# Retention and PReLU MLP on one core: fewer bytes of loads under way at first, one weight piece finished by halves, the last output block sent by quarters

## The chip, the cores and the metric

The kernel runs on one core of one Trainium2 chip. A core has a matrix engine (PE in the profile; PEld is its weight load), three elementwise engines (DVE, ACT, POOL), SyncE (SP), which here only starts transfers, and 16 DMA engines between the chip's main memory and the on-chip SBUF. Matmul results go to PSUM, a small memory that POOL does not read in this kernel. The metric is the device time of one execution in microseconds (us): 1020.53 us, the median of three runs from 1019.59 to 1022.61. The profile is of a fourth execution of 1020.18 us; its span, from the first to the last instruction, is 1018.5 us, and all instants below count from the span's start.

## The reference

```python
# q, k, v: (8, 8, 576, 64) float32
scores = matmul(q, k.T) / sqrt(64)
gamma  = 1 - 2.0 ** (-5 - arange(8))                 # one decay per head
Dmat   = where(i >= j, gamma ** (i - j), 0)          # per head, 576 x 576
x      = matmul(scores * Dmat, v)                    # then (B,H,S,D) -> (4608, 512)
h = x @ w_in                                         # w_in (512, 2048), float64
g = maximum(h, 0) + alpha * minimum(h, 0)            # alpha (2048,)
out = g @ w_out                                      # w_out (2048, 512), float64; out float32
```

## The kernel before

**Retention.** It is computed in chunks of 64 positions: within a chunk by masked scores, across chunks by a running sum of k-times-v states that decays by gamma. The powers of gamma are tables built at the start on DVE. Batch 0, the first 576 tokens, is handled in three parts of 256, 256 and 64 tokens, all eight heads at once, by the `part_*` functions; the other batches go by pairs of heads.

**MLP.** The 4608 tokens form 18 blocks of 256. A block goes through 8 units; unit i makes two 128-row pieces of h (matmuls into `ph`), applies the PReLU into `g`, and adds `g` times the rows of w_out into the block's output sums in PSUM (`po`, `mlp_out`). Blocks 0 and 1 are "plain" (L412 `plain_unit`, L390 `plain_out`). The other 16 use seven products of half-size operands instead of eight, from sums of weights and of x (L451 `mlp_unit`, L380). When a block's last unit is in, `out_block` (L355) combines the seven sums into the four 128x256 quarters `osb[m][x]` of the output and sends each 128-token row m as one 256 KB transfer (L369 to L371).

**Weights.** Both weights are float64 and are turned into float32 on the chip by 32 pieces, in the order in which the units use them: for unit i two pieces of w_in (each of two loads of 256 KB) and two of w_out (one load of 512 KB each). Pieces 0 and 1 together hold unit 0 of w_in; piece 2 and 3 its rows of w_out. `piece_in` (L285) runs two ACT instructions on a loaded piece (L296, L298); `piece_out` (L301) runs three DVE instructions through one PSUM buffer `c` (L307, L310, L312) and one on POOL (L314), and asks for the next load (`fetch`).

**Loads.** Nearly all loads are started by SP, which works through its list in order. `load` (L77) makes a load wait until the one that lies `in_flight` bytes back in the list has landed: it adds sizes backwards from the new load, itself included, and waits for the first earlier load before which the sum has reached the limit. The limit is 5 x 256 KB at first (L90), 7 x 256 KB from L827 on, and none from L889 on. The list begins with k and v of part 0 (two loads of 256 KB each), pieces 0 to 5, k, q, v of part 1 (six of 256 KB), then, under the second limit, pieces 6 and 7 and part 2. The two loads of part 0's q and the small alpha go out on ACT's queue (L161, L167) and are not counted.

**Order.** From L134 to L942 every engine runs its instructions in the order in which the code calls for them. Around the change it is (L830 to L863): scale, transpose and score part 0; `piece_in(1)`; states of part 0 (four ACT copies at L744, three POOL sums at L746); `piece_in(2)`; `piece_out(2)`, which is where pieces 0 and 1 are finished; the values of part 0 (PE at L764 and L775, then six ACT copies at L781 and L783 that fill `xb[0]`, the first three of them its first half); `piece_out(1)`; `piece_in(2)`, `piece_out(1)`; `plain_unit(0, 0)`. The last makes 8 matmuls at L419, each of which the trace shows as two: the first four use piece 0 and the first half of `xb[0]`, the next two the first half of piece 1, the last two its second half. Later the order of each engine comes from a scheduler.

Of the kernel before, what the change touches and what calls it, by code (L numbers as in the profile page):

```python
# [10 lines left out]
FP32 = mybir.dt.float32  # L11
INT32 = mybir.dt.int32
UINT32 = mybir.dt.uint32
ACTF = mybir.ActivationFunctionType
ALU = mybir.AluOpType
# [3 lines left out]
def kernel(  # L19
# [10 lines left out]
    nc = tc.nc  # L30
# [3 lines left out]
    P = 128  # L34
# [9 lines left out]
    HM = DM // 2  # L44
    TB = 2 * P
    NKB = NTOK // TB
# [40 lines left out]
                ahead += n  # L87
            flight.append((ins, size))

    in_flight = [5 << 18]  # L90

# [99 lines left out]
    for i in range(NBIT - 1):  # L193
        nc.vector.scalar_tensor_tensor(out=dif[:, i + 1], in0=dif[:, i], scalar=2.0,
                                       in1=dif[:, i], op0=ALU.add, op1=ALU.mult)
# [6 lines left out]
                            op=ALU.mult)  # L202
    nc.vector.tensor_scalar(pf, pf, 1.0, None, ALU.add)

    for o, x, y in ((slice(0, 2), slice(0, 2), slice(3, 5)), (0, 0, 1), (0, 0, 2), (1, 0, 5)):
# [7 lines left out]
                                   in1=pf[:, 6], op0=ALU.mult, op1=ALU.mult)  # L213
# [17 lines left out]
    for h2 in range(2):  # L231
# [6 lines left out]
                                       in1=tabx[hd, :, 0], op0=ALU.add, op1=ALU.mult)  # L238
# [13 lines left out]
    HI_MAX = float(np.array([0x47EFFFFF], np.uint32).view(np.float32)[0])  # L252
    HI_MIN = float(np.array([0x38000000], np.uint32).view(np.float32)[0])
# [10 lines left out]
    def fetch(n):  # L264
        while npiece[0] < min(n, len(pieces)):
            srcs, at = pieces[npiece[0]][0], npiece[0]
            npiece[0] += 1
            free[:] = [t for t in free if at < gone.get(t, len(pieces))]
            t = free.pop(0)
            if isinstance(t, str):  # L270
                raw = ring.tile([P, 4 * HM], INT32, tag=t, name=f"raw_{at}")
            else:
                raw = w_in[t][:, 4:6].rearrange("p s u c f -> p (s u c f)").bitcast(INT32)
            for i, src in enumerate(srcs):
                to = raw
                if len(srcs) > 1:
                    to = raw.rearrange("p (x e f two) -> p x e f two", x=2, e=2, two=2)[:, :, i]
                load(to, src, P * 4 * HM * 4 // len(srcs))
            raws.append((raw, t))
# [21 lines left out]
    def piece_out(n):  # L301
        for _ in range(min(n, len(half_done))):
            at, a, lo, hi, t = half_done.pop(0)
            dst = pieces[at][1]

            c = ps_h.tile([P, 2, HM], INT32, tag="psh1", name=f"wc_{at}")
            nc.vector.tensor_scalar(c.bitcast(FP32), a, HI_MIN, HI_MAX, ALU.max, ALU.min)  # L307


            nc.vector.tensor_scalar(c, c, 3, 0x3FFFFFF8,  # L310
                                    ALU.logical_shift_left, ALU.bitwise_and)
            nc.vector.scalar_tensor_tensor(out=dst.bitcast(INT32), in0=hi, scalar=-0x40000000,  # L312
                                           in1=c, op0=ALU.bitwise_and, op1=ALU.bitwise_or)
            nc.gpsimd.tensor_tensor(out=dst.bitcast(INT32), in0=dst.bitcast(INT32), in1=lo,  # L314
                                    op=ALU.add)
            free.append(t)
            fetch(at + 1 + AHEAD)

# [36 lines left out]
    def out_block(kb, po):  # L355
        p1, p2, p6, p7, p5, p3, p4 = [po[n // 2][:, n % 2, :] for n in range(7)]

        osb = ring.tile([P, 2, 2, HM], FP32, tag=f"o{kb % 2}", name=f"osb_{kb}")
        s12 = wraw.tile([P, 2, HM], FP32, tag="wa", name=f"s12_{kb}")
        u3 = wraw.tile([P, HM], FP32, tag="wa", name=f"u3_{kb}")  # L360
        s1, u2 = s12[:, 0], s12[:, 1]
        nc.scalar.copy(s1, p1)
        for o, x, y, op in ((osb[:, 0, 0], p2, s1, ALU.add), (u2, p6, s1, ALU.add),
                            (u3, p7, u2, ALU.add), (s1, p5, u2, ALU.add),
                            (osb[:, 1, 1], p5, u3, ALU.add),
                            (osb[:, 0, 1], p3, s1, ALU.add)):
            nc.vector.tensor_tensor(out=o, in0=x, in1=y, op=op)
        nc.vector.tensor_tensor(out=osb[:, 1, 0], in0=p4, in1=u3, op=ALU.add)
        for m in range(2):  # L369
            t0 = kb * TB + m * P  # L370
            nc.sync.dma_start(out[t0:t0 + P, :], osb[:, m].rearrange("p x f -> p (x f)"))  # L371

    def mlp_out(between=None):
        kb, i, g = pend.pop(0)
        if kb in PLAIN:
            return plain_out(kb, i, g, between)
        if i == 0:
            acc[kb] = [ps_o.tile([P, 2, HM], FP32, tag=f"pso{n}", name=f"po{n}_{kb}")
                       for n in range(4)]
        for n, (x, y) in enumerate(PROD):  # L380
            nc.tensor.matmul(acc[kb][n // 2][:, n % 2, :], g[:, x, :], w_out[i][:, y, :],  # L381
                             start=(i == 0 and n % 2 == 0),
                             stop=(i == NU - 1 and (n % 2 == 1 or n == 6)),
                             skip_group_check=True)
        if i == NU - 1:
            out_block(kb, acc.pop(kb))
# [449 lines left out]
    part_states(0)  # L836
    piece_in(2)
    piece_out(2)
    part_carry(0)
    part_values(0)  # L840
    aps = ps_a.tile([P, NFC], FP32, tag="psa", name="aps")
    nc.tensor.transpose(aps, a16, ident[0:NFC, 0:NFC])
    piece_out(1)
    nc.vector.tensor_copy(alpha, aps)
    nc.vector.tensor_scalar(nalpha, alpha, -1.0, None, ALU.mult)
    piece_in(2)
    piece_out(1)
    part_scale(1, 1)
    plain_unit(0, 0)
# [97 lines left out]
    for b in range(2, B):  # L947


        nq, first, at = len(queue), b * NPAIR, {}  # L950
# [56 lines left out]
```

## Time and profile before

| what | value |
|---|---|
| PE busy | 1001.3 us, 98% of the span |
| DVE, ACT, POOL busy | 778.3, 269.4, 179.2 us |
| DMA | 64.30 MB, mean 63 GB/s; up to 238 GB/s in a fortieth of the span |
| PE in the forty slices | 0.6 busy in the first, 0.7 in the last, 0.9 or more in each between |
| chain that ended last | PE 94%, DVE 3%, DMA 1% |
| output transfers | 36 of 256 KB, median 2.3 us from issue to landing |

The page gives busy time per engine, the span in forty slices, the DMA queues, the chain of work that ended last (followed back from the end, at each step to what released it), and the costliest groups of instructions. Since PE is busy nearly everywhere from about 42 us to the last block, a query of the trace by stages is needed to see the beginning and the end, which is where the change acts. `in_flight` and the order of pieces only matter while weights are being loaded; the tail is what lies behind the last matmul.

### The profile page before, as it was taken

What the parts mean: (1) busy time and instruction counts of PE and PEld (TensorE: products, weight loads), DVE (VectorE), ACT (ScalarE), POOL (GpSimd) and SP (SyncE); (2) the same over time, 40 slices, a digit from 0 to 9 for tenths busy, and PEclk for the clock granted to TensorE, in tenths of its full rate; (3) what the DMA queues carried; (4) which work ended last, traced back from release to release, by engine and by line L of the source; (5) the groups of instructions that cost most, each with busy time, mean ns of one, the idle gap of its engine ahead of it and who ended that gap; (6) DMA issues with size and microseconds to landing.
All of it is one profiled execution on the core that took longest, in us unless ns stands there. A gap on an engine that the chain in (4) does not pass through costs nothing.

```text
span 1018.5 us, 23084 instructions
## 1 busy us (share of the span) xinstructions
PE 1001.3 (98%) x9385; PEld 894.2 (88%) x9385; DVE 778.3 (76%) x2086; ACT 269.4 (26%) x605; POOL 179.2 (18%) x201
## 2 busy tenths in 40 slices
PE   6999999999999999999999999999999999999997
PEld 5666668899999999999999999999999999999997
DVE  6669966878887888768778788887878777667665
ACT  4556653223222222122021312232222211000000
POOL 5656674300100020100010000200020001010000
PEclk8999999999999999999999999999999999999999
DMA  9975744322231323112112313222313000000000
GB/s 238 238 194 140 185 74 103 60 60 48 52 64 40 63 37 69 25 45 48 44 25 56 60 45 60 57 48 54 62 45 60 13 23 1 22 1 21 2 21 22
DMA packets 229308, 64.30 MB, mean 63 GB/s; under 512 B 214337, under 2 KB 222545, under 8 KB 229201
## 3 DMA queue, kind: packets, MB, share of 16 engines
q1 hardware_dynamic: 227088, 62.29, 27.1%
q8 instruction: 74, 1.21, 0.5%
q10 hardware_dynamic: 2112, 0.53, 0.3%
q14 instruction: 34, 0.27, 0.1%
HBM read 53.35 MB, written 9.44 MB: 62 GB/s over the span
## 4 chain that ended last, share of the span: by engine, by line
PE 94%; DVE 3%; DMA 1%; ACT 0%; issue 0%; SPq 0%; POOL 0%; DVEq 0%; ACTq 0%
PE ph L463 38%; PE po L381 37%; PE ph L419 6%; PE po L398 6%; PE pv L656 3%; PE ps L614 1%; PE ps L620 1%; DMA w_out<-in_k_dram 1%; PE ph L614 1%; DVE su L589 0%; DVE g L476 0%; PE pt L697 0%; DVE mt L636 0%; PE ps L716 0%; PE ps L556 0%
## 5 line engine op out<-in xcount | busy, mean ns | idle before, releaser
L381 PE MATMUL po<-w_out,g 128*128 128x256 f32 x1792 | 410.9, 381 | 0.2
L381 PEld LDWEIGHTS po<-w_out,g 128*128 128x128 f32 x1792 | 330.1, 190 | 42.7 <-DVE g L487 1.3
L476 DVE TENSOR_TENSOR g<-ph,g 128x256 f32<-128x256 f32 (+1 forms) x512 | 187.0, 386 | 127.2 <-ACT g L471 75.2
L463 PE MATMUL ph<-xb,w_in 128*128 128x128 f32 x2048 | 272.7, 276 | 0.0
L463 PEld LDWEIGHTS ph<-xb,w_in 128*128 128x128 f32 x2048 | 257.1, 192 | 7.9 <-issue 0.7
L463 PE MATMUL ph<-xt,w_in 128*128 128x128 f32 x1536 | 213.8, 275 | 0.7 <-DVE g L476 0.7
L463 PEld LDWEIGHTS ph<-xt,w_in 128*128 128x128 f32 x1536 | 192.2, 192 | 1.1 <-PE ph L463 0.8
L487 DVE TENSOR_TENSOR g<-g 128x128 f32<-128x128 f32 x512 | 127.2, 289 | 5.4
L471 ACT COPY g<-ph 128x128 f32<-128x128 f32 x128 | 34.1, 266 | 327.7 <-PE ph L463 217.1
L528 POOL TENSOR_TENSOR qx<-qx,tabx 128x576 f32<-128x576 f32 x28 | 32.3, 1153 | 379.6 <-DMA qx<-in_q_dram 223.4
L481 DVE SCALAR_TENSOR_TENSOR g<-g 128x512 f32<-128x512 f32 x128 | 91.3, 714 | 3.8
L479 DVE TENSOR_SCALAR g<-g,alpha 128x256 f32<-128x256 f32 x256 | 84.3, 370 | 2.8
L597 ACT COPY vn<-su 64x512 f32<-64x512 f32 x56 | 34.6, 617 | 135.2 <-DVE su L591 134.5
L419 PE MATMUL ph<-xb,w_in 128*128 128x256 f32 x256 | 61.7, 397 | 0.8 <-POOL w_in L314 0.8
L419 PEld LDWEIGHTS ph<-xb,w_in 128*128 128x128 f32 x256 | 50.1, 198 | 11.0 <-issue 2.4
L398 PE MATMUL po<-w_out,g 128*128 128x512 f32 x128 | 58.6, 599 | 0.9 <-DVE g L435 0.9
L625 DVE SCALAR_TENSOR_TENSOR mt<-ph,th,mask 64x64 f32<-64x64 f32 x48 | 13.6, 283 | 52.5 <-PE ph L614 52.2
L665 ACT COPY xb<-pv 128x256 f32<-128x256 f32 (+3 forms) x84 | 22.7, 321 | 109.8 <-PE pv L656 109.8
L636 DVE SCALAR_TENSOR_TENSOR mt<-ps,th,mask 64x256 f32<-64x256 f32 x96 | 46.1, 481 | 2.3
L533 ACT ACTIVATE vn<-vn,tabv 64x576 f32<-64x576 f32 x56 | 43.3, 774 | 8.7 <-DMA vn<-in_v_dram 7.8
L398 PEld LDWEIGHTS po<-w_out,g 128*128 128x128 f32 x128 | 23.4, 190 | 24.5 <-issue 22.9
L589 DVE SCALAR_TENSOR_TENSOR su<-su,gch 128x64 f32<-128x64 f32 x84 | 43.1, 513 | 2.1
(134 smaller groups left out, 717.0 us busy)
## 6 DMA issues: line engine op xcount, KB each, us to landing
out_dram<-osb SPq DMA_DIRECT2D x36, 256.0 KB, 2.3
kx<-in_k_dram SPq DMA_DIRECT2D x112, 72.0 KB, 2.6
qx<-in_q_dram SPq DMA_DIRECT2D x112, 72.0 KB, 3.0
vn<-in_v_dram SPq DMA_DIRECT2D x56, 144.0 KB, 3.2
kn<-in_k_dram SPq DMA_DIRECT2D x56, 144.0 KB, 3.3
raw<-in_moe_w_in_dram SPq DMA_DIRECT2D x24, 256.0 KB, 4.5
raw<-in_moe_w_out_dram SPq DMA_DIRECT2D x10, 512.0 KB, 5.4
w_in<-in_moe_w_out_dram SPq DMA_DIRECT2D x6, 512.0 KB, 5.7
```

Of the source, the lines that this page charges most:

```text
L381: nc.tensor.matmul(acc[kb][n // 2][:, n % 2, :], g[:, x, :], w_out[i][:, y, :], start=(i == 0 and n % 2 == 0), stop=(i == NU - 1 and (n % ...
L398: nc.tensor.matmul(acc[kb][m], g[:, 2 * x + m], w_out[i][:, 2 * x:2 * x + 2].rearrange("p x f -> p (x f)"), start=(i == 0 and x == 0), sto ...
L419: nc.tensor.matmul(ph[:, x], w_in[i // UST][:, cc // 2 * 2 + x, i % UST, cc % 2], xb[kb][:, cc], start=(cc == 0 and x == 0), stop=(cc == N ...
L463: nc.tensor.matmul(ph[m][:, o], w_in[i // UST][:, l, i % UST, cc], r[:, cc], start=(n in (0, 3) and cc == 0), stop=(n in (2, 6) and cc == ...
L476: nc.vector.tensor_tensor(out=o, in0=x0, in1=x1, op=ALU.add)
L479: nc.vector.tensor_scalar(g[:, 4 + 2 * m:6 + 2 * m], g[:, 2 * m:2 * m + 2], 0.0, alpha[:, fc:fc + 1], ALU.min, ALU.mult)
L481: nc.vector.scalar_tensor_tensor(out=g[:, 0:4].rearrange("p x t -> p (x t)"), in0=g[:, 0:4].rearrange("p x t -> p (x t)"), scalar=0.0, in1 ...
L487: ins = nc.vector.tensor_tensor(out=g[:, o, :], in0=g[:, x0, :], in1=g[:, x1, :], op=op)
L533: nc.scalar.activation(vn[x, h2], vn[x, h2], ACTF.Copy, scale=tabv[x, c:c + 1])
L589: nc.vector.scalar_tensor_tensor(out=su[:, j], in0=su[:, j - 2], scalar=g2, in1=su[:, j], op0=ALU.mult, op1=ALU.add)
L597: nc.scalar.copy(vn[half(h2), h2, 1:], su[half(h2)])
L636: nc.vector.scalar_tensor_tensor(out=mt[to, h2, p2:NJ - 1:2], in0=ps[p2][half(x), 0], scalar=th[to, 3, h:h + 1], in1=mask[to, None, :].to_ ...
```

## The change

It has three parts. The limit on loads under way at first becomes 3 x 256 KB (0.75 MB) instead of 1.25 MB; the later limit is the same. Piece 1 is finished by its two column halves, so that a matmul may wait for the half that it uses: three DVE instructions and one of POOL become six and two of half the size. The last block's four quarters each go out as soon as they are there, as 128 KB transfers, two on SP's queue and two on ACT's, instead of two rows of 256 KB on SP's. The first two are for the beginning, so that what is needed first has less beside it and the first matmuls of the MLP wait for less; the third is for the end.

```diff
-    in_flight = [5 << 18]
+    in_flight = [3 << 18]
...
             c = ps_h.tile([P, 2, HM], INT32, tag="psh1", name=f"wc_{at}")
-            nc.vector.tensor_scalar(c.bitcast(FP32), a, HI_MIN, HI_MAX, ALU.max, ALU.min)
-            nc.vector.tensor_scalar(c, c, 3, 0x3FFFFFF8,
-                                    ALU.logical_shift_left, ALU.bitwise_and)
-            nc.vector.scalar_tensor_tensor(out=dst.bitcast(INT32), in0=hi, scalar=-0x40000000,
-                                           in1=c, op0=ALU.bitwise_and, op1=ALU.bitwise_or)
-            nc.gpsimd.tensor_tensor(out=dst.bitcast(INT32), in0=dst.bitcast(INT32), in1=lo,
-                                    op=ALU.add)
+            for f in (slice(0, P), slice(P, HM)) if at == 1 else (slice(0, HM),):
+                dst_e, c_e, a_e, hi_e, lo_e = [y[:, :, f] for y in (dst, c, a, hi, lo)]
+                nc.vector.tensor_scalar(c_e.bitcast(FP32), a_e, HI_MIN, HI_MAX, ALU.max, ALU.min)
+                nc.vector.tensor_scalar(c_e, c_e, 3, 0x3FFFFFF8,
+                                        ALU.logical_shift_left, ALU.bitwise_and)
+                nc.vector.scalar_tensor_tensor(out=dst_e.bitcast(INT32), in0=hi_e,
+                                               scalar=-0x40000000, in1=c_e,
+                                               op0=ALU.bitwise_and, op1=ALU.bitwise_or)
+                nc.gpsimd.tensor_tensor(out=dst_e.bitcast(INT32), in0=dst_e.bitcast(INT32),
+                                        in1=lo_e, op=ALU.add)
...
         nc.vector.tensor_tensor(out=osb[:, 1, 0], in0=p4, in1=u3, op=ALU.add)
+        if kb == NKB - 1:
+            for (m, x), eng in (((0, 0), nc.sync), ((1, 1), nc.scalar), ((0, 1), nc.sync),
+                                ((1, 0), nc.scalar)):
+                t0 = kb * TB + m * P
+                eng.dma_start(out[t0:t0 + P, x * HM:(x + 1) * HM], osb[:, m, x])
+            return
         for m in range(2):
```

Each engine's order of instructions is the same in both kernels but for these: six DVE and two POOL instructions in place of three and one, and the four output transfers. What changes beyond them is what SP's early loads wait for.

## The prediction

> **What bounds the kernel now.** I read the page's busy times first, then the slices, the chain of waits, stages of the beginning, and the tail.
>
> ```profile
> PE 1001.3 (98%) x9385; PEld 894.2 (88%) x9385; DVE 778.3 (76%) x2086; ACT 269.4 (26%) x605; POOL 179.2 (18%) x201
> ...
> PE   6999999999999999999999999999999999999997
> ```
>
> PE is the bound: 1018.5 - 1001.3 leaves 17 us without PE, and the slices put them at the two ends. From 60 to 110 us the stages show PE busy 50.00 of 50 us. So a microsecond that PE gains or loses in the first 40 us reaches the end whole, and so does one behind the last matmul; nothing else counts. The chain of waits over the first 120 us, and the timeline of the first 60:
>
> ```profile
> 1.31 5.78 DMA w_out<-in_k_dram
> 17.89 1.29 POOL w_in L314
> 19.18 0.08 issue
> 19.26 6.76 PE ph L419 x16
> 34.36 3.65 PE ph L419 x16
> ```
> ```profile
> 17.13 1.21 PE L775 MATMUL pv<-pT,w_out 64*32 64x64 f32 x82 [2.13 <-issue]
> 17.96 0.37 ACT L781 COPY xb<-pv 128x256 f32<-128x256 f32 x1 [1.47 <-PE pv L775]
> 18.37 0.74 ACT L783 COPY xb<-pv 64x256 f32<-64x256 f32 x2
> ```
>
> Three things are seen. The same 16 matmuls of L419 take 6.76 us at 19.26 and 3.65 us at 34.36. Before them PE stands 2.13 us (15.00 to 17.13) for nothing that the profile shows. And L419 is charged to piece 1 (POOL, 19.18), but ACT's copies of the first half of `xb[0]`, which the first matmul needs as well, end at 18.37 + 0.74 = 19.11. The first matmul uses piece 0, which POOL finished at 17.31. So I hold the copies, not piece 1, for the releaser. The stages say why L419 is slow (columns: stretch, its length, PE, PEld, DVE, ACT, POOL busy, granted clock, DMA share, GB/s):
>
> ```profile
> 15.20:18.62 3.42, 1.37 (x83) 1.17 (x82) 3.10 (x6) 1.92 (x5) 2.77 (x4) 1.00 0.91 308
> 18.62:22.03 3.41, 2.77 (x7) 2.26 (x8) 2.61 (x6) 3.33 (x9) 2.44 (x3) 0.50 1.00 251
> 22.03:25.45 3.42, 3.42 (x10) 2.70 (x9) 1.09 (x2) 0.61 (x2) 2.17 (x2) 0.50 0.98 215
> 25.45:28.86 3.41, 2.50 (x14) 1.71 (x13) 1.66 (x4) 2.82 (x6) 1.12 (x2) 1.00 0.98 282
> ```
>
> The clock is halved from 18.62 to 25.45, 6.83 us, after a stretch in which PE was busy 1.37 of 3.42 us. The tail, from the timeline of the end:
>
> ```profile
> 1013.98 0.41 DVE L368 TENSOR_TENSOR osb<-po,u 128x256 f32<-128x256 f32 x1
> 1014.09 1.08 SPq L371 DMA_DIRECT2D out_dram<-osb  x2
> ```
>
> The last sum ends at 1014.39, the second row's issue starts at 1014.83 and lands at 1017.36 (2.53 us); 1.1 us of final barriers follow.
>
> **What the Trainium skill says.** (1) "TensorE: Matmul & The Clock Gate", Part 1: the matrix clock is halved when an activity monitor finds the engine idle, in free-running windows of 3413 ns, so that the instant varies from run to run. The trace agrees: both changes lie on a grid of 3.41 us, 6.83 us apart. (2) "Runtime: NRT & Kernel Launch", Instruction fetch mechanics: each engine fetches its instructions by a DMA queue of its own in 16 KiB blocks of 256, mostly hidden. Here it seems not to be hidden: the page has 74 instruction packets of 1.21 MB on q8; a packet of 16,384 bytes runs from 14.79 to 15.75, and PE resumes 1.38 us later. PE's only other wait of this kind ends at 40.59, 1.49 us after the end of such a packet. (3) "DMA: Bandwidth & Descriptors", Issuing engines are not separate DMA queues: a second issuing engine saves the sequencer's issue time only. The trace has it as 0.33 us for each of the last two issues.
>
> **Part 1, the limit.** It removes nothing from SP's list; each 256 KB load now waits for the third before it instead of the fifth. The first three loads are unaffected, and in the records the bytes of both k loads and both q loads are in by 6.9 us, with less than 0.04 MB of v among them. So the first chain (k at 7.08, q at about 7.9, POOL scaling, transposes, scores at 10.11) gains nothing; I charge 0. Then I rebuilt the landings from the trace's own times: 1.0 us from an issue to its first bytes, 0.75 us from last bytes to landing, 256 KB in 0.73 us at about 350 GB/s (the stretch 10 to 14 shows 341), 512 KB in 1.6. Before against after: piece 0, 11.73 and 11.75; piece 1, 13.19 and 13.5 (its second load waits for piece 0's first, 10.95, instead of v's first, 9.15); piece 2, 15.25 and 16.15; piece 3, 17.90 and 17.8; pieces 4 and 5, 19.35 and 19.45, 20.86 and 21.3; part 1's last q, 25.2 and 25.9; its last v, 27.75 and 28.2; piece 6, 29.57 and 29.8. Queued behind each waiting issue are SP's later loads, which this includes. What uses them: ACT takes piece 1 at 14.05, piece 2 at 15.28, and is then free from 16.50 until PE gives it `pv` at 17.94. Piece 2 at 16.15 keeps ACT to 16.15 + 0.66 + 0.66 = 17.4, hidden. All later ones have from 1 to 5 us. Lateness therefore costs 0; if piece 2 came at 17.2 or later, ACT would reach its copies later than now, some 0.5 us.
>
> The gain is the fetch. With three loads of 0.73 us under way and a round trip of 1.0 + 0.73 + 0.75 = 2.5 us, the queues run nearly dry at times; by my rebuilding no data moves from 12.8 to 13.8. The packet now runs beside a full queue and takes 0.96 us. The request for it is not shown; if it comes near 12.7, when PE has gone through some 256 of its instructions, it waited 2.1 us, where a load on an empty queue took 1.1. I take it 1.0 us earlier and 0.3 us shorter, bounds 0 and 1.5: PE resumes at about 15.8 instead of 17.13 and is done with L775 at 17.0. ACT is free at 17.4, so its copies start 0.5 us earlier than at 17.96, and L419 at about 18.75.
>
> That half microsecond may count more than once. Unless PE is busy enough, the clock stays halved for another window: 2.77 of 3.41 us (81%) from 18.62 to 22.03 was too little. Starting at 18.75 it is 3.28 of 3.41 (96%), and the full window 22.03 to 25.45 was enough. So I expect the full clock from 22.03: of 16 matmuls at 0.427 us (6.83/16), 7.7 run slowly, and 8.3 at 0.216 take 1.8 us; the group ends at 23.9 to 24.0 instead of 26.02. Head: -2.0 us. Behind it the scaled q of part 1 would be ready at 25.85 + 1.04 = 26.9, needed at 27.6 (29.58 - 2.0), and the other loads above still precede their use, so none of it is given back.
>
> **Part 2, the halves.** DVE: six instructions at some 0.39 us (L479 and L367, 128x256, took 0.370 and 0.42) for three at 0.69: +0.25 us. POOL: two at 0.73 (L746, 128x256) for one of 1.28, but the first may start at 17.31, before DVE has done the second, so piece 1 is ready at about 18.9 instead of 19.17, its first half at 18.1. Behind it on DVE stands piece 2, 0.25 us later, which PE needs only at 27.79. Piece 1 is needed by the fifth matmul, some 1.7 to 3.4 us after the first. So it is worth 0 to 0.1 us now: hidden by the first four matmuls.
>
> **Part 3, the quarters.** The last quarter is issued at 1014.43 on ACT's idle queue, where SP's second row began at 1014.83, and carries 128 KB: 0.37 us less. Against it stands the ACT queue's own start: its first q load, issued at 0.80, showed bytes at 2.9, SP's first at 1.9. Gain 0.4 + 0.37 less up to 1.0; bounds -0.1 and 0.9, taken 0.5 us.
>
> **Sum.** -2.0 - 0.5 = -2.5: 1018.0 us.
>
> **The rivals.**
> A (0.40), the forecast: 1018.0.
> B (0.27), the fetch isn't helped, or the clock's window falls otherwise; only the tail and part of the half microsecond are left: -0.5 to -1.2, about 1019.6. For it: the request's instant isn't shown, and the packet may not have waited for data.
> C (0.20), PE's shorter standstill keeps the clock from being halved at all: 6.83/2 = 3.4, and 0.5 and 0.5: -4.4, some 0.7 given back where piece 6 (needed at 27.8) comes 2 us late for ACT: -3.7, about 1016.8. Against it: PE still stands from 17.0 to 18.75.
> D (0.13), slower: loads come later than I rebuilt, piece 2 past 17.2 and all behind it by 1 to 2 us; L419 starts 0.5 us late and the clock is halved for a window more (1.7), less the tail's 0.5: +1.7, about 1022.2, with +3.4 if two windows are lost.
>
> **How the numbers follow.** The three runs of before spread over 3 us, which a free-running window would do; each case spreads by some 1.5 us. 0.3% is 3.06 us, so faster by more takes C and two fifths of A and little of B: 0.43. Slower by more is a third of D and stray: 0.09. Within 0.3%: 0.48. The range from 1015.0 to 1021.8 leaves out the far half of C's spread and most of D.
>
> **What would show it.** The packet on q8 starting before 14 us and PE's standstill before L775 under 1.5 us; L419 first at 18.5 to 18.9; the granted clock full from about 22; `raw` loads of piece 2 landing at 16 to 16.5; the last issue at 1014.4 or, with the head's gain, 2 us earlier, and under 2.5 us to landing. It is wrong if the first copies of `xb[0]` still start at 17.96 or later, or if ACT waits for piece 2.

## The result, and the profile after

The changed kernel takes 1023.65 us (median of six runs, 1022.18 to 1025.94) where the kernel before took 1019.78 beside it. The ratio is 1.0035, 95% interval 1.0019 to 1.005: by this ratio slower by 3.6 us, in place of the 2.5 us gained that were forecast, and outside the range. The profile shown is of the run of 1025.94 us, the slowest of the six, so its sizes are larger than the median's; where the excess lies is shown below. Line numbers are a few higher in the changed kernel: what was L314 is L318, L367 is L371 and L368 is L372 (the sums of the last block), L371 is L378 (its last transfer), and after that each is 11 higher (L419 is L430, L697 is L708).

The page of the changed kernel, busy time and slices:

```profile
PE 1003.1 (98%) x9385; PEld 893.9 (87%) x9385; DVE 779.4 (76%) x2089; ACT 269.4 (26%) x605; POOL 179.4 (18%) x202
...
PE   5799999999999999999999999999999999999998
```

PE's work is the same and 1.8 us longer busy; the span is 5.7 us longer. The loss is in the first two slices (6 and 9 before, 5 and 7 now). In the stages, PE is busy 18.19 of the first 30 us (19.89 before), 10.82 from 30 to 45 (13.96 before), and 50.00 of 50 from 60 to 110 in both. The chain of waits over the first 120 us, in order of time (start, length, what):

```profile
10.21 3.66 DMA raw<-in_moe_w_in_dram
...
13.89 3.48 DMA w_in<-in_moe_w_out_dram
...
17.39 3.55 DMA raw<-in_moe_w_in_dram
...
21.01 3.43 DMA raw<-in_moe_w_in_dram
...
24.45 3.79 DMA w_out<-in_q_dram
...
35.64 3.64 issue
39.28 5.86 PE ph L430 x14
...
53.18 7.10 PE ph L430 x32
```

Before, no load stood in this chain after 7 us: it ran over PE, then over DVE and POOL on pieces 0 and 1, and was PE's almost alone from 19.26 on. Now loads that wait for loads carry it to 28 us, one round trip of 3.4 to 3.8 us behind the other. The last line, two groups of L430 in a row, started at 46.97 before: 6.2 us are lost by then. From there to the end of PE's last matmul the two profiles differ by less than 1 us (966.5 before, 967.2 now; 966.4 to 967.2 in all twelve profiles of this document), and behind the last sum the changed kernel gains 1.2 us.

The timeline of the first 60 us at the place that the prediction was about:

```profile
16.18 1.21 PE L786 MATMUL pv<-pT,w_out 64*32 64x64 f32 x82 [1.55 <-issue]
...
17.39 0.67 ACT L296 ACTIVATE wa<-w_in 128x512 f32<-128x512 f32 x1 [1.42 <-DMA w_in<-in_moe_w_out_dram]
...
18.52 0.35 ACT L792 COPY xb<-pv 128x256 f32<-128x256 f32 x1
...
19.77 5.38 PE L430 MATMUL ph<-xb,w_in 128*128 128x256 f32 x16 [2.23 <-ACT xb L794]
```

PE's standstill before the value matmuls did shrink, from 2.13 to 1.55 us, and ended at 16.18 instead of 17.13. But ACT now waits 1.42 us for piece 2, which landed at 17.37, and reaches the copies into `xb[0]` at 18.52 instead of 17.96. PE waits for these copies, as the profile now says itself. ACT, POOL and PE a little later:

```profile
36.59 0.66 ACT L296 ACTIVATE wa<-raw 128x512 f32<-128x512 f32 x1 [4.71 <-DMA raw<-in_moe_w_out_dram]
...
37.71 1.04 ACT L736 COPY w_out<-ps 128x512 f32<-128x512 f32 x2
...
38.35 2.50 POOL L737 TENSOR_TENSOR w_out<-w_out,mask 128x512 f32<-128x512 f32 x2 [3.29 <-ACT w_out L736]
...
39.28 5.86 PE L430 MATMUL ph<-xb,w_in 128*128 128x256 f32 x14 [3.64 <-issue]
...
45.07 1.16 PE L775 MATMUL pv<-w_out,w_out 64*64 64x64 f32 x64
```

ACT stands 4.71 us for piece 6, whose load was issued at 28.68 (24.12 before) and landed at 36.51 (29.57). Behind it on ACT stand the copies of part 1's scores, which ran at 33.53 before and run at 37.71 now, and POOL's masks behind them. But PE loses nothing by it here: the masks are done at 40.85, and PE begins part 1's values at 45.07, right behind its group of L430.

PE stands for another reason. It stops at 35.64, after two of the group's 16 matmuls, and goes on at 39.28, and the profile names no releaser. (POOL had finished piece 5, the last that the group needs, at 35.06.) A packet of 16,384 bytes of instructions runs on q8 from 36.15 to 37.59. In six other profiles below PE stops at the same place, for 0.86 to 1.39 us, and in all seven it goes on 1.65 to 1.89 us after the end of such a packet. In the six the packet starts 1.1 to 1.3 us ahead of the group, in this one 1.2 us behind its start: some 2.4 us later, which is about what this execution lies above the median (2.3 us). Whether the other five executions had it is not recorded.

So the 6.2 us divide as follows, by PE's idle time and by the half-clock time up to the third group. Standstills without a releaser: 5.19 us in place of 2.89. The wait for the copies into `xb[0]`: 2.23 in place of 0.76. All other waits after 9 us: 2.69 in place of 1.46. The halved clock: some 1.2 us more, by an estimate that takes half of PE's busy time at half clock as lost (4.32 us in place of 3.09). In this run the clock came down twice (stretch, length, PE, PEld, DVE, ACT, POOL busy, granted clock, DMA share, GB/s):

```profile
20.62:24.04 3.42, 3.42 (x10) 2.70 (x9) 2.63 (x6) 2.64 (x5) 1.56 (x2) 0.50 0.72 227
24.04:37.69 13.65, 9.55 (x159) 5.86 (x158) 5.35 (x9) 5.68 (x10) 7.61 (x7) 1.00 1.06 226
37.69:44.52 6.83, 5.24 (x12) 4.22 (x13) 5.26 (x10) 2.27 (x5) 4.87 (x4) 0.50 0.94 286
```

The tail, timeline of the end:

```profile
1020.72 1.02 ACTq L378 DMA_DIRECT2D out_dram<-osb  x2
1020.94 0.42 DVE L372 TENSOR_TENSOR osb<-po,u 128x256 f32<-128x256 f32 x1
```

The last sum ends at 1021.35, the last quarter is issued on ACT's queue at 1021.38 and lands at 1023.25: 1.90 us from sum to landing, where it was 2.97.

### The profile page after: what moved, and what is told of

Read it like the earlier page. It is cut to its first block, busy times and chain, and to the rows that moved or that the text cites. A ratio compares the mean times of both kernels' runs of the same rounds, so it can differ in the third digit from the quotient of the medians.

```text
span 1024.2 us, 23094 instructions
## 1 busy us (share of the span) xinstructions
PE 1003.1 (98%) x9385; PEld 893.9 (87%) x9385; DVE 779.4 (76%) x2089; ACT 269.4 (26%) x605; POOL 179.4 (18%) x202
## 4 chain that ended last, share of the span: by engine, by line
PE 93%; DMA 3%; DVE 3%; issue 1%; ACT 0%; POOL 0%; SPq 0%; DVEq 0%; ACTq 0%; POOLq 0%
PE ph L474 38%; PE po L392 37%; PE ph L430 5%; PE po L409 5%; PE pv L667 3%; PE ps L625 1%; DMA raw<-in_moe_w_in_dram 1%; PE ps L631 1%; DMA w_out<-in_v_dram 1%; PE ph L625 1%; DVE su L600 0%; DVE g L487 0%; DMA w_out<-in_k_dram 0%; DMA w_out<-in_q_dram 0%; DVE mt L647 0%
## 5 line engine op out<-in xcount | busy, mean ns | idle before, releaser
L392 PEld LDWEIGHTS po<-w_out,g 128*128 128x128 f32 x1792 | 329.8, 190 | 43.7 <-DVE g L498 2.5
L608 ACT COPY vn<-su 64x512 f32<-64x512 f32 x56 | 34.5, 616 | 136.5 <-DVE su L602 135.8
L430 PE MATMUL ph<-xb,w_in 128*128 128x256 f32 x256 | 63.1, 403 | 5.9 <-issue 3.6
L430 PEld LDWEIGHTS ph<-xb,w_in 128*128 128x128 f32 x256 | 50.8, 202 | 16.8 <-issue 6.4
L460 POOL TENSOR_TENSOR xt<-xb 128x256 f32<-128x256 f32 x16 | 11.7, 730 | 187.1 <-PE ph L474 187.1
```

The lines of the kernel that those rows point to most:

```text
L430: nc.tensor.matmul(ph[:, x], w_in[i // UST][:, cc // 2 * 2 + x, i % UST, cc % 2], xb[kb][:, cc], start=(cc == 0 and x == 0), stop=(cc == N ...
L608: nc.scalar.copy(vn[half(h2), h2, 1:], su[half(h2)])
```

## The experiments

**Theories.** Theory 1: the lower limit alone makes the loss, because a load's round trip is 3.4 us and more, so that three loads under way don't fill the DMA engines, everything behind falls late, and ACT and PE wait for it. Theory 2: the halves' extra DVE work and the clock's windows make it. Theory 3, for the second series: any other limit than 5 shifts waits and costs the same. Four kernels ran beside the kernel before in the first series (its median there 1019.05 us), four in the second (1019.19), two in the third (1019.26). Differences are ratios of one series; 0.1% is 1.0 us.

### The limit alone

```diff
-    in_flight = [5 << 18]
+    in_flight = [3 << 18]
```

> Only the first limit is lowered, from 5 x 256 KB to 3 x 256 KB; pieces and output are as in the kernel before. Theory 1 (late loads): with three loads under way and a round trip of 3.2 to 3.8 us in the trace after, the loads of part 1 and piece 6 come 4 to 7 us late, ACT waits for piece 2 and piece 6, and PE loses what the change lost and the tail gave back: 3.9 + 1.2 = 5.1 us slower than before, 4 to 7; piece 2 lands near 17.4 and piece 6 past 34 us. Theory 2 (the halves and the clock's windows cost it, the late loads are hidden): within 1 us of before.

1023.51 us, ratio 1.0045 (1.0029 to 1.0061): 4.6 us slower. Piece 2 landed at 17.02, piece 6 at 33.15. As theory 1 expects, but for piece 6, which was less late than expected and than in the profile after. Without halves and quarters the whole loss is there, so theory 2 falls.

### The limit put back, halves and quarters kept

```diff
-    in_flight = [3 << 18]
+    in_flight = [5 << 18]
```

> The changed kernel with the first limit put back to 5 x 256 KB. Theory 1: the halves are hidden behind the first four matmuls, so only the tail remains: 1.2 us faster than before (0.6 to 1.6). Theory 2: the six DVE instructions of 0.43 us for three of 0.69 put 0.5 us before piece 2 and everything behind it on DVE, and a later first group of matmuls costs clock windows: 2 to 4 us slower than before.

1017.90 us, ratio 0.9989 (0.9983 to 0.9996): 1.1 us faster than before. In its profile the six half-size DVE instructions take 0.43 us each as in the profile after, and nothing waits for them on PE.

### The quarters alone

```diff
         nc.vector.tensor_tensor(out=osb[:, 1, 0], in0=p4, in1=u3, op=ALU.add)
+        if kb == NKB - 1:
...
+            return
```

> Only the last block's output is changed, to four quarters on two queues. Both theories: the last landing is 1.9 us after the last sum, as in the trace after, where it was 2.97 us before, and the closing barriers are the same: 1.2 us faster than before (0.6 to 1.6). If ACT's idle queue started slowly, as the forecast allowed, 0 to 0.5.

1017.99 us, ratio 0.9985 (0.9978 to 0.9993): 1.5 us faster. Last sum to landing is 1.91 us (1012.44 to 1014.35); it is 1.89 to 1.91 in all profiles with the quarters but one (2.70, `second_limit5` below). With the run before it: the halves are worth nothing that these intervals can tell (0.9989 against 0.9985).

### The lower limit for part 0 and pieces 0 and 1 only

```diff
+    fetch(2)
+    in_flight[0] = 5 << 18
     fetch(6)
     load_part(1)
```

> The changed kernel, but the limit of 3 x 256 KB holds only for the loads of part 0 and of pieces 0 and 1; from piece 2 on it is 5 x 256 KB as before. Theory 1: piece 2 no longer waits for piece 1 but goes out behind it, lands at 15.5 to 16.5, and the later loads are at most 1 us later than before; the instruction packet is still early; 1 to 2 us faster than before, of which the tail is 1.2. Theory 2: as the changed kernel, 3 to 4 us slower than before.

1019.54 us, ratio 1.0003 (0.9995 to 1.0011). Both expectations missed, theory 1's by 1.3 us or more: piece 1's first load, issued at 10.38, landed only at 14.10, and piece 2 at 17.61, so the first group of matmuls started at 20.02. A few late loads are enough to make what follows them late. Why piece 2 took 5.93 us from its issue, though the higher limit held for it, is not shown. Later loads recovered (piece 6 at 31.07), and most of the loss with them.

### Other limits

The first limit at 4 and, in another kernel, at 7 (`[7 << 18]`), all else as in the changed kernel:

```diff
-    in_flight = [3 << 18]
+    in_flight = [4 << 18]
```

> The changed kernel with the first limit at 4 x 256 KB. Theory 1 (a load takes 3.4 to 3.7 us from issue to landing, so n loads under way bring n x 256 KB in that time: 3 give 215 to 230 GB/s, 4 give 290 to 310, 5 are held by the engines' own 340): loads late by about a third of what they are at 3; 0 to 1 us slower than before with the tail's 1.2 in it, so 1 to 2 us slower than the same kernel at 5. Theory 3 (any limit below what the list had been laid out for shifts the waits for semaphores and costs the same): as the changed kernel, 4 to 5 us slower than before.

> The changed kernel with the first limit at 7 x 256 KB. Theory 1: from 5 on the engines are full, so more loads under way bring nothing sooner: as with 5, 1.2 us faster than before, within 0.5. Theory 3: slower than with 5 by some us. If the instruction packet waits for the data queue (the forecast), PE stands longer before its value matmuls, up to 1 us, and the gain shrinks to 0.5.

At 4: 1019.17 us, ratio 1.0001 (0.9992 to 1.001). At 7: 1018.38 us, ratio 0.9989 (0.9982 to 0.9996), the same as at 5. So the cost grows step by step below 5, and 7 brings nothing more, which is what theory 1 expects and theory 3 does not.

Theory 1's arithmetic missed, though: it had 290 to 310 GB/s at 4, and 238 moved from 12 to 28 us. A load's time is not fixed. From piece 4 to part 1's last v a load of 256 KB took on average 3.7 us from issue to landing at 3, 4.5 us at 4, and 4.8 us in the kernel before. With these, 3, 4 and 5 loads under way make 211, 233 and 272 GB/s, against 223, 238 and 267 in the traces. PE's standstill before the value matmuls, which was to be up to 1 us longer at 7, was 2.29 us, against 1.53 at 5 with halves and quarters and 2.13 before.

ACT's wait for piece 6 does not follow the loss: it is 2.79 us at 4 (the timeline below), 1.89 with the limit alone, 4.71 in the profile after.

```profile
32.44 0.67 ACT L296 ACTIVATE wa<-raw 128x512 f32<-128x512 f32 x1 [2.79 <-DMA raw<-in_moe_w_out_dram]
```

### The lower limit up to piece 5

```diff
     fetch(6)
+    in_flight[0] = 5 << 18
     load_part(1)
```

> The changed kernel, but the limit is back at 5 x 256 KB after pieces 0 to 5, ahead of part 1's k, q and v. Theory 1: piece 2 is as late as in the changed kernel (17.4), so the first group of matmuls starts at 19.5 to 19.8; part 1's loads go out with two more under way, so piece 6 lands 2 to 3 us sooner, near 33 us, and ACT waits for it little: 1 to 2.5 us slower than before. If the lateness of piece 2 alone makes the loss: 3 to 4 us slower, as the changed kernel.

1022.69 us, ratio 1.0038 (1.0026 to 1.005): 3.9 us slower, as the changed kernel. Theory 1's 1 to 2.5 us are missed; the figure is that of the other case, that piece 2 alone makes the loss, which the next run tests. In the trace part 1's loads did not make up for the delay: by piece 5 the list was 5 us late (20.86 before, 25.76 here), and it stayed so (part 1's last v at 32.89, 27.75 before). PE stands 2.14 us before 27.13 for part 1's k. With the limit lowered up to piece 1 only, the ratio was 1.0003, against 0.9989 at 5 throughout: pieces 0 and 1 under the limit cost 1.4 us, pieces 2 to 5 some 3.5 us more. In the 8 runs of this kernel the granted clock has the same mean as in the 38 runs of the kernel before (0.9969): this loss is not the clock's.

### ACT's work on piece 2 moved behind the copies

The changed kernel, but ACT takes piece 2 after part 0's values, so that a late piece 2 no longer stands ahead of the copies into `xb[0]`:

```diff
-    piece_in(2)
+    piece_in(1)
     piece_out(2)
     part_carry(0)
     part_values(0)
+    piece_in(1)
```

> The changed kernel with the two ACT instructions on piece 2 called after the values of part 0 instead of ahead of them, so that ACT's copies into xb no longer stand behind a late piece 2; loads as in the changed kernel. Theory 1: the first group of matmuls starts near 18.5 to 18.8 instead of 19.77, but piece 6 and part 1 are as late as before, and what is won is lost again there: 3 to 4 us slower than before, at most 1 us better than the changed kernel. If piece 2 alone makes the loss: 1 us faster than before.

1022.51 us, ratio 1.0036 (1.0018 to 1.0053). Its timeline, PE alone:

```profile
19.03 3.72 PE L430 MATMUL ph<-xb,w_in 128*128 128x256 f32 x16 [1.20 <-POOL w_in L318]
26.40 2.31 PE L708 MATMUL pt<-ident,w_out 128*128 128x128 f32 x8 [3.65 <-DMA w_out<-in_k_dram]
```

The case of piece 2 alone expected 1 us faster than before, so it falls. This profile fell on a full clock for the first group: done at 22.75, 3.3 us earlier than before the change (26.02). PE then stood 3.65 us for part 1's k, which landed at 26.27. In this execution a gain at this place, larger than the prediction hoped for, is taken back in full by late loads.

### Two tries for a better kernel

The limit at 4 for part 0 and pieces 0 and 1, then 7; and the limit at 5 both at first and later (where it was 7):

```diff
-    in_flight = [3 << 18]
+    in_flight = [4 << 18]
...
+    fetch(2)
+    in_flight[0] = 7 << 18
     fetch(6)
```
```diff
-    in_flight = [3 << 18]
+    in_flight = [5 << 18]
...
-    in_flight[0] = 7 << 18
+    in_flight[0] = 5 << 18
     fetch(8)
```

> The changed kernel with the limit at 4 x 256 KB for part 0 and pieces 0 and 1 only, and at 7 x 256 KB from piece 2 on. Theory 1: pieces 0 and 1 are at most 0.5 us later than at 5, which is hidden, piece 2 lands before 16 us and nothing behind it is late; as with 5 throughout, 1.2 us faster than before, and up to 1 us better if the instruction packet comes as early as it did at 4 (13.2 instead of 14.4 to 14.8) and the first group of matmuls starts at 18.5. Theory 3: as with 4 throughout, equal to before.

> The changed kernel with the first limit at 5 x 256 KB and the second, for pieces 6 on and part 2, also at 5 instead of 7. Theory 1: pieces 6 and 7 are 512 KB each, so 5 x 256 KB lets them out behind one load more; they land 0.5 to 2 us later, ACT waits that much more for piece 6; 0 to 1 us slower than with 7, that is 0 to 1.2 us faster than before. If the second standstill for an instruction packet (0.9 us near 32) comes from the queue being full there, it shrinks and the kernel gains up to 0.9 us instead.

The first: 1018.38 us, ratio 0.9995 (0.9986 to 1.0003), not told apart from the kernel before where 1.2 us faster was expected; the instruction packet came at 15.22, not at 13.2. The second: 1018.89 us, ratio 0.9991 (0.9983 to 0.9999), about as with 7: its profile has no standstill near 32, but piece 7 came at 35.45 and ACT waited for it 2.7 us. Neither beats the old limits with the quarters.

### The kernels in one table

From each profile's records: GB/s from 12 to 28 us, landings of piece 2, of part 1's last v and of piece 6, the start of the third group of plain_unit's matmuls (all in us), and the ratio to the kernel before.

| first limit (x 256 KB) | GB/s | piece 2 | last v | piece 6 | third group | ratio |
|---|---|---|---|---|---|---|
| 5, kernel before | 267 | 15.25 | 27.75 | 29.57 | 46.90 | 1 |
| 7, halves, quarters | 285 | 14.41 | 26.25 | 29.96 | 46.25 | 0.9989 |
| 5, quarters | 271 | 15.19 | 27.55 | 29.57 | 44.98 | 0.9985 |
| 5, halves, quarters | 258 | 14.88 | 28.09 | 30.51 | 44.64 | 0.9989 |
| 5, and 5 later, not 7 | 243 | 15.08 | 28.77 | 30.54 | 45.73 | 0.9991 |
| 4 to piece 1, then 7 | 269 | 15.70 | 27.90 | 29.48 | 45.45 | 0.9995 |
| 4, halves, quarters | 238 | 16.30 | 29.45 | 32.36 | 46.79 | 1.0001 |
| 3 to piece 1, then 5 | 256 | 17.61 | 29.71 | 31.07 | 47.27 | 1.0003 |
| 3 to piece 5, then 5 | 207 | 17.19 | 32.89 | 34.18 | 50.67 | 1.0038 |
| 3, piece 2 behind | 214 | 17.77 | 32.20 | 33.84 | 50.15 | 1.0036 |
| 3, changed kernel | 223 | 17.37 | 32.31 | 36.51 | 53.11 | 1.0035 |
| 3, limit alone | 228 | 17.02 | 31.10 | 33.15 | 48.69 | 1.0045 |

All but the first and the last row have the quarters' gain in their ratio, about 1.5 us. The ratio, of many runs, goes with the lateness of part 1's last v, of one profile each: with the quarters it is below 1 up to 28.8 us, 1 near 29.5, and 1.0035 and more above 32. The GB/s order the kernels less well (243 with 0.9991). The third group's start is of single profiles, each with its own clock; that of the kernel at 5 with halves and quarters ran with the clock never halved up to there, that of the kernel before with 6.83 us at half.

## Why the prediction was wrong

**What bounds the kernel.** Right: PE, with the beginning and the tail the only places that count, and what was lost by 53 us stayed lost up to the tail. Right too that ACT's copies, not piece 1, release the first group: the profile after names them, as do the profiles at 5 and 7 with the quarters. Both signs that the prediction gave for its being wrong came: ACT waited for piece 2, and the first copies of `xb[0]` started later than 17.96, at 18.52.

**The step that failed: the landings rebuilt under the new limit.** The prediction put an issue's first bytes at 1.0 us, 256 KB at 0.73 us, last bytes to landing at 0.75: 2.5 us. Part 0's first k load shows such a start (1.11 us), and w_in's first loads in the full queue before show such bytes and landings (0.80 to 0.93 and 0.71 to 0.73 us). In the changed kernel, for pieces 4 and 5 and part 1, the records have 1.4 us to the first bytes of a load that found the queue empty (up to 2.3 behind another), 1.0 to 1.6 us of bytes, and 0.6 to 1.3 us to landing: 3.4 to 4.4 us, 3.7 on average. (Which bytes are a load's is taken from the order of issue.) By the forecast's 2.5 us three loads of 256 KB would have made 315 GB/s; by 3.7 us they make 211, and the stretch from 12 to 28 us shows 223, against 267 before. The landings, by the same terms:

| | before | forecast | measured |
|---|---|---|---|
| piece 0, second load | 11.73 | 11.75 | 12.53 |
| piece 1, second load | 13.19 | 13.5 | 14.55 |
| piece 2 | 15.25 | 16.15 | 17.37 |
| piece 5, second load | 20.86 | 21.3 | 24.44 |
| part 1, last q | 25.22 | 25.9 | 29.45 |
| part 1, last v | 27.75 | 28.2 | 32.31 |
| piece 6 | 29.57 | 29.8 | 36.51 |

Each late landing lets the next load out late, so the error grows along the list, from 0.8 us to over 4. The prediction had named the edge itself, piece 2 at 17.2, and the rival that lies behind it (D, with 0.13, 1022.2 us). That rival has the right direction and path, but its sum is too small: it had the later loads 1 to 2 us late where they were 4 to 7, and put the rest on a further clock window.

**"None of it is given back" fell with it.** The later loads were to have 1 to 5 us to spare; part 1's k, q and v and piece 6 used that up and more.

**The packet of instructions.** Right in time: forecast at about 13.8, measured 13.76, and between 13.76 and 14.10 in the four profiles where the limit of 3 holds at that time, against 14.41 to 14.80 in those that begin with 5 or 7. That a shorter queue brings the packet sooner is supported, not shown: each is a single profile, the kernel at 4 has it earliest of all (13.19), and from 12.8 to 13.8, where the forecast had no data moving, 246 GB/s moved. So that the instant came out right was in part luck. Its length did not shrink (0.96 us), and PE resumed at 16.18 instead of 15.8. In eleven profiles PE resumes 1.27 to 1.48 us after the packet's end, and in the twelfth PE doesn't stand there; this supports the reading that the standstill is for instructions, but no run takes the packet away. A gain of 0.95 us at this point was real and worth nothing, because ACT came later for another reason. The prediction counted the packet that gains and not the next one: in the profile after, PE's second such standstill is its longest wait behind the first loads.

**The clock.** The rise at 22.03 was built on the phase of one profile. The grid moved: from 20.62 to 24.04 it was halved here, then from 37.69 to 44.52 after PE's 3.64 us of standstill. In the profiles of the two kernels with the old limits and the quarters, the clock was not halved between its first rise and the tail. As an average over runs it can't be forecast from one profile. Its part in the 3.6 us was not measured by itself. The mean granted clock is 0.9955 in the changed kernel's six runs and 0.9971 in 52 runs of the kernel before: 0.0016 of 1022 us, 1.6 us of PE's work at most (an estimate). Among those 52 runs 0.001 less clock goes with 0.3 us more, which would make it 0.5 us. The kernel with the limit of 3 up to piece 5 loses 3.9 us without such a difference.

**The halves.** Right in kind: hidden. DVE took 0.43 us an instruction, not 0.39 (2.7 us for six with their gaps against 2.2 for three).

**The quarters.** Right in kind, too small: 0.5 forecast. The last sum's landing came 1.07 us sooner in the profile after, and alone they bring 1.5 us (0.7 to 2.2). Of the 1.07 us, 0.41 are the earlier issue (0.03 us after the last sum, where it was 0.44) and 0.66 the shorter way from issue to landing (1.87 for 2.53), for which 0.37 were forecast. The subtraction of up to 1.0 us for ACT's queue starting slowly had no ground here: its last quarter landed 1.87 us after its issue, SP's last 1.83 us after its own. In one of ten profiles with the quarters ACT's last took 2.67 us.

**Sum by the runs.** Limit +4.6, quarters -1.5, halves about 0: +3.1, against +3.6 measured (1.9 to 5.1).

**What stays open.** Why piece 6, once issued, took 7.8 us in the profile after and 4.7 to 6.7 in the profiles of the experiments: of the 16 steps of its landing 15 had come by 34.16, and the last came at 36.51. Whether that and the late instruction packet have one cause is not shown. And how the median's loss divides: in the profiles of the five kernels with the limit of 3 up to piece 5 or throughout, or with 4, no wait of PE from 34 us to the third group is put down to piece 6 or the masks; there are only standstills without a releaser (0.5 to 3.6 us at a time) and short waits for `xb` (0.3 to 0.4). The loss up to there goes by the wait for `xb[0]` in some and by part 1's loads in others, and each profile is one execution.

## What to carry to other kernels

A limit on bytes under way has to cover a round trip as it is under that limit. One put together from landings in a full queue came out too short here (2.5 us for 3.7), the round trip grew with the number of loads under way, and a list of loads that wait for each other adds up every shortfall. Before crediting a gain at one wait, look at the in-order engine that stands between it and the next: here ACT, with a load's work queued ahead of the copies that PE needed. Where a profile names no releaser for a long wait, look for an instruction packet that ends shortly before it. At the end of a kernel, sending each finished part at once, on two queues, was the one part of this change that paid; smaller parts and the second queue were not tried apart.

## What was not expected of the hardware

- A 256 KB load of w_in took 3.43 us from issue to landing (issued at 21.01), its bytes moving for 1.4 us, most of that time alone, where loads in a full queue moved theirs in 0.76 to 0.95 us one behind the other. That is 185 GB/s against the 341 of the stretch from 10 to 14 us before.
- Rows of 256 bytes do not move at one speed: in the profile after, part 1's ran at 18 to 22 ns a packet from 24 to 31 us, part 2's at 41 to 51 ns from 34.5 to 36; from 34 to 36 us only 177 GB/s moved with the DMA share at its maximum. The same slowing is in the kernel before from 30 us on.
- A kernel's runs spread by several us: 52 runs of the kernel before span 1016.70 to 1022.95, and their granted clock from 0.995 to 1.0.
